# Decay attention with a soft mixture of experts on one core: score tiles of 64x128, row-group sums in 128x32 tiles, C's transposes as filler

## Chip, cores and metric

One core of one Trainium2 chip. The metric is device time in microseconds (us) of one execution; of several executions the median is given.

## What is computed

Four batches, 8 heads of 64 columns, 768 positions, all in f32. For each head and each block of positions the reference computes

    intra = (q k^T * Dmask) v          Dmask[i, j] = lam^(i-j) for i >= j
    inter = (q * lam^(pos+1)) kv_state
    out   = intra + inter
    kv_state = lam^block * kv_state + (k * lam^(block-1-pos))^T v

and then, with x the attention output as 3072 rows of 512 columns, a soft mixture of 8 experts with 4 slots each:

    logits = x phi                                   (3072 x 32)
    d = softmax of logits over the rows, slot_input = d^T x   (32 x 512)
    slot_out[e] = relu(slot_input[e] w1[e]) w2[e]    (w1: 512 x 1024, w2: 1024 x 512 per expert)
    c = softmax of logits over the slots, result = c slot_out

## The kernel before

The host only lays the inputs out. The kernel works with blocks of 128 positions: 24 tiles t (6 per batch), taken as 12 pairs u = (a, b) by the loop at L482. Every engine runs its instructions in the order in which the code is written (`InOrder`), and nearly all of them carry the line of that helper, L48; so the profile is read by the names of tiles.

One pair, on TensorE (PE), in this order: `scores(a)` (q k^T of 8 heads: 16 matmuls into banks sc0 and sc1), `recall(a)` (the state's part: 8 matmuls into xa and xb, from `qs` and `st`), `scores(b)` (banks tr and dp), `recall(b)`, `natural` of the two tiles before (8 transposes), `turn_k` (up to 8 transposes of k), in every second pair `weights` (2 transposes), `attend` (masked scores times v: 8 matmuls into xa, then 8 into xb), `gathered` (k^T v for the state: up to 16 matmuls into bank kv), and then `logits` (odd pairs, 16 matmuls) or `slots` (even pairs, 4). VectorE (DVE) masks the scores (`at`) and carries the state (`st`); GpSimd (POOL) makes `qs`, the decayed state `dec` and `vd`; ScalarE (ACT) copies results out of PSUM. A matmul of f32 is run as two passes: two matmul records and two weight loads in the trace; a transpose is one of each.

Tiles of the array: a matmul with 64 rows of contraction and 64 output columns uses a quarter of the array, and four such run beside each other; the scores and the recall are both of this form (64*64 in the trace). `natural` and `turn_k` are 128*128, `attend` and `gathered` 128*64, `logits`, `slots` and both expert layers 128*32 (four expert groups beside each other), the last products with C 32*128 (four row groups).

Loads are issued by SyncE (SP) alone: the q, k, v tiles of pair u+2 during pair u (14 buffers `ld`), and between them 3.4 tiles of w1 per pair (512 KB each, 32 buffers `slab`); w2 follows as buffers come free.

After the last pair comes a chain (L570 to L767) with filler transposes `busy(n)`, which do no work and stand where PE would wait: the maximum over the four row groups of 32 partitions (`cm`, a matmul with `blk`, a 128x128 tile made of four copies of `sel`), the slot weights `selw`, the slot inputs `si` (8 matmuls into one bank, then three transposes by DVE into `e`), `first(Q)` for the two halves of the experts (32 matmuls each, kc by kc; `between` is called after the second of four kc), the softmax denominators `den`, the last group of C (`lp`, `slot_softmax`, then six transposes `turn_C` inside `first(1)`), and the second layer: `second(0)` and `second(1)` with 16 calls of `quad` each (4 matmuls). Into `second(1)` are put `spread(0)` (the slot outputs of the first 256 columns, summed over row groups with `blk`) before quad `AT_SPREAD`, and three `put` (8 matmuls with C for 1024 rows each, copied out by ACT and DVE and stored) before the quads `AT_PUTS`. Then `spread(1)` and three `put` of the second half end the kernel. `put` takes its four banks from a list of seven in turn.

    AT_SPREAD = 2
    AT_PUTS = (5, 9, 13)

Of the kernel before, what the change touches and what calls it, by code (L numbers as in the profile page):

```python
# [8 lines left out]
F32 = mybir.dt.float32  # L9
# [19 lines left out]
HD = D // 2  # L29
NU = T // 2  # L30

AT_SPREAD = 2
AT_PUTS = (5, 9, 13)
AHEAD = 20
PACE = 34

# [17 lines left out]
def decay_attn_soft_moe(  # L54
# [153 lines left out]
    def scores(t, tags):  # L208
        q_, k_ = IN[t, 0], IN[t, 1]
        SC[t] = [bank(tag) for tag in tags]  # L210
        for hp in range(HP):
            for j in range(2):
                for hh in range(2):
                    r = slice(64 * hh, 64 * hh + 64)
                    pe.matmul(
                        out=SC[t][hh][64 * j:64 * j + 64, hp * P:(hp + 1) * P],
                        lhsT=k_[r, hp * P + 64 * j:hp * P + 64 * j + 64],
                        rhs=q_[r, hp * P:(hp + 1) * P],
                        start=True,
                        stop=True,  # L220
                    )
        AT[t] = []

    def masked(t, hh):
# [63 lines left out]
                    skip_group_check=True,  # L288
                )

    def attend(ts, xt):
        for hh in range(2):
            for t in ts:
                v_ = IN[t, 2].rearrange("p (h c) -> p h c", h=H)
                for hp in range(HP):
                    pe.matmul(
                        out=place(t, hh, hp),
                        lhsT=v_[:, HP * hh + hp, :],
                        rhs=AT[t][hh][:, hp, :],
                        start=False,  # L300
                        stop=True,
                        skip_group_check=True,
                    )
            banks, at = XB[ts[0]]
            n = 2 * P * len(ts)
            act.copy(
                out=xt[:, ts[0] % 2:ts[-1] % 2 + 1, 2 * hh:2 * hh + 2],
                in_=banks[hh][:, at:at + n].rearrange("p (t a b) -> p t a b", t=len(ts), a=2),
            )
        for t in ts:  # L310
            XT[t] = xt[:, t % 2]
# [20 lines left out]
    def carry(t, kv):  # L332

        if not has_state(t):
            return
        n = t % NB
        st = work.tile([P, HP, DH], F32, tag="st", name="st", bufs=2)
        if n == 0:
            dve.tensor_copy(out=st, in_=kv)
        else:  # L340
            dve.tensor_tensor(out=st, in0=DEC[t - 1], in1=kv, op=ALU.add)
        ST[t] = st
# [135 lines left out]
        dve.tensor_reduce(out=gsel, in_=ident.rearrange("p (g s) -> p g s", g=4), axis=AX.X, op=ALU.add)  # L478

    ask = sm = late_sums = iter(())  # L480
    kv = None
    for u in range(NU):  # L482
        a, b, c = 2 * u, 2 * u + 1, 2 * u + 2
        opens, last = a % NB == 0, u == NU - 1
        feed(u)
        if u == NU - 2:
            for _ in range(NLOAD - 6):
                load_one(*ld1)
        if last:
            for tag, n in (("kn", 2), ("vd", 1)):  # L490
                for _ in range(n):
                    load_one(work, tag, n)

        scores(a, ("sc0", "sc1"))
        if u > 0:
            carry(a, kv[:, 1])
            decay_state(a)
        masked(a, 0)
        masked(a, 1)
        xb = [bank("xa"), bank("xb")]  # L500
        XB[a], XB[b] = (xb, 0), (xb, 2 * P)
        if u == 0:
            decay_v(0)
            decay_q(1)
            turn_k(0, "gl", True)
            scores(b, ("tr", "dp"))
            kv = gathered((0,))
            carry(0, kv[:, 0])
            decay_state(0)
            masked(b, 0)  # L510
            masked(b, 1)
            turn_k(b, "sc0", True)
            turn_k(c, "sc1", False)
            decay_v(b)
            decay_q(c)
            recall(b, True)
        else:
            if not opens:
                recall(a, True)
            scores(b, ("tr", "dp"))  # L520
            masked(b, 0)
            masked(b, 1)
            recall(b, opens)
            next(ask, None)
            next(ask, None)
            next(late_sums, None)
            decay_v(b)
            if u == 1:
                place_phi()
            decay_q(c)  # L530
            natural(a - 2, "sc0")
            natural(a - 1, "sc1")
            if not last:
                turn_k(b, "tr", True)
                turn_k(c, "dp", False)
            if u % 2 == 0:
                sm = slot_softmax(u // 2 - 1, weights("gl"))
                next(sm)
            decay_q(c + 1)
        xt = keep.tile([P, 2, HP, P], F32, tag="xt", name="xt", bufs=2)  # L540
        attend((a, b), xt)
        next(sm, None)
        if u == 0:
            constants()
        if not last:
            kv = gathered((b, c))
            carry(b, kv[:, 0])
            decay_state(b)
            if u == 0:
                decay_q(c + 1)  # L550
        next(sm, None)
        if u % 2 == 1:
            ask = logits(u // 2)
            next(ask)
            if not last:
                next(ask)
        elif u > 0:
            late_sums = slots(u // 2 - 1)
            next(late_sums)
# [7 lines left out]
    for _ in range(2):  # L567
        load_two(keep, "xt", 2)

    def busy(n):  # L570

        idle = bank("tr")
        for _ in range(n):
            pe.transpose(idle[:, 0:P], ident, ident)

    negm = run["m"]
    blk = work.tile([P, 4, SL], F32, tag="st", name="blk", bufs=2)
    blk_ = blk.rearrange("p g s -> p (g s)")
    pool.tensor_copy(out=blk, in_=sel.rearrange("p (o s) -> p o s", o=1).broadcast_to([P, 4, SL]))
    dve.tensor_scalar(out=gm, in0=gsel, scalar1=negm, scalar2=None, op0=ALU.mult)  # L580
    natural(T - 2, "tr")
    next(ask)
    natural(T - 1, "dp", dve.tensor_copy)
    cm = bank("kv")
    pe.matmul(out=cm[:, 0:4], lhsT=blk_, rhs=gm, start=True, stop=True)
    weights("xb", raw=False, copy=dve.tensor_copy)
    busy(6)
    dve.tensor_reduce(out=own, in_=cm[:, 0:4], axis=AX.X, op=ALU.min)
    wgt = small.tile([P, 1], F32, tag="mx", name="wgt")
    act.activation(out=wgt, in_=negm, func=AF.Exp, bias=own, scale=-1.0)  # L590
# [2 lines left out]
    pool.tensor_scalar(out=selw, in0=sel, scalar1=wgt, scalar2=None, op0=ALU.mult)  # L593
    late_sums = slots(G - 1, ("sc0", "sc1"))
    next(late_sums)
    busy(2)
    next(late_sums)
    for _ in range(4):
        load_one(keep, "x", 4)

    si = bank("xa")
    for half in range(2):
        for kc in range(4):
            pe.matmul(
                out=si[SL * kc:SL * kc + SL, half * DH:(half + 1) * DH],
                lhsT=selw,
                rhs=acc[:, half * HD + kc * DH:half * HD + (kc + 1) * DH],
                start=True,
                stop=True,
            )  # L610

    busy(4)
    sT = e.rearrange("p (a b) -> p a b", a=4)
    for cols in (slice(0, SL), slice(SL, DH), slice(DH, P)):
        dve.transpose(out=e[:, cols], in_=si[:, cols])
    next(ask)
    wl = small.tile([P, 1], F32, tag="rs", name="wl")
    dve.tensor_tensor(out=wl, in0=wgt, in1=lsum, op=ALU.mult)
# [1 line left out]
    rown = small.tile([P, 2], F32, tag="rown", name="rown", bufs=1)  # L620

    def denominators():
        den = bank("kv")
        pe.matmul(out=den[:, 0:1], lhsT=blk_, rhs=wl, start=True, stop=True)
        dve.tensor_scalar(out=rden, in0=den[:, 0:1], scalar1=1e-9, scalar2=None, op0=ALU.add)
        dve.reciprocal(out=rden, in_=rden)

        dve.tensor_tensor(out=rown, in0=own2, in1=rden.broadcast_to([P, 2]), op=ALU.mult)
# [59 lines left out]
            quad(d_, Q, f, w, n == 0, n == len(todo) - 1)  # L688

    first(0, denominators)  # L690
    lp = bank("dp")[:, 0:P]
    pe.transpose(lp, L, ident)
    while late:
        load_two()
    for x in slot_softmax(G - 1, lp):
        pass
    CT = slabs.tile([P, G, P], F32, tag="slab", name="CT")

    def turn_C():

        tops = [bank("sc0"), bank("sc1")]
        for g in range(G):
            pe.transpose(
                tops[g // 3][:, (g % 3) * P:(g % 3 + 1) * P],
                CN[:, 4 * g:4 * g + 4, :].rearrange("p g s -> p (g s)"),
                ident,
            )
        for i, copy in enumerate((act.copy, dve.tensor_copy)):
            copy(out=CT[:, 3 * i:3 * i + 3, :], in_=tops[i][:, 0:3 * P].rearrange("p (a b) -> p a b", a=3))

    first(1, turn_C)

    so = work.tile([P, D], F32, tag="at", name="so", bufs=4)
    po1 = bank("xa")
# [10 lines left out]
    def spread(half):  # L725

        rep = bank(("gl", "xb")[half])
        pe.matmul(out=rep[:, 0:HD], lhsT=blk_, rhs=so[:, half * HD:(half + 1) * HD], start=True, stop=True)
        x = slabs.tile([P, HD], F32, tag="slab", name="s4")
        split(x, rep)  # L730
        s4.append(x)
# [25 lines left out]

    second(0, po, {})
    split(so[:, 0:HD], po)
    fill = {AT_SPREAD: lambda: spread(0)}  # L760
    for i, n in enumerate(AT_PUTS):
        fill[n] = lambda i=i: put(i, 0)
    second(1, po1, fill)
    split(so[:, HD:D], po1)
    spread(1)
# [59 lines left out]
```

## Time and profile before

| | |
|---|---|
| median of 3 runs | 164.79 us (164.21 to 165.23) |
| the profiled execution, its own time | 164.39 us |
| its span, first to last instruction | 162.6 us |
| mean granted TensorE clock, share of full | 0.987 |
| PE busy | 146.9 us (90%) |
| HBM read, written | 52.50 MB, 6.29 MB |

The span leaves 1.8 us of the profiled execution outside. PE is PE's matmuls, PEld its weight loads. A matmul record lasts longer than the distance to the next one, since they are pipelined; what the stream costs is read from the starts. "issue" names time in which an engine waited for nothing that the profile shows.

### The profile page before, as it was taken

The numbers are of one execution on the slowest core, as the hardware profiler recorded it, in microseconds if no ns is written. First come the engines' busy times: TensorE is split into PE (matmuls) and PEld (weight loads), VectorE is DVE, ScalarE is ACT, GpSimd is POOL, SyncE is SP. The second block draws the span as 40 slices with busy tenths as digits, with TensorE's granted clock in tenths as the row PEclk, the third lists the DMA queues.
The fourth block names the chain that finished last, engine by engine and source line by source line (L and its number), as shares of the span: only waits on it lengthen the run. The fifth ranks groups of instructions, "written<-read, shape, count | busy, mean of one in ns | idle before, by whom it ended". The sixth has DMA issues, their size and how long they took to land.

```text
span 162.6 us, 6432 instructions
## 1 busy us (share of the span) xinstructions
PE 146.9 (90%) x2768; PEld 111.6 (69%) x2768; DVE 81.3 (50%) x184; ACT 49.2 (30%) x112; POOL 48.7 (30%) x64
## 2 busy tenths in 40 slices
PE   7899996999699999999799999999999999996900
PEld 7688995799597888689779998885333365552600
DVE  1994544573835747573657385735117140334620
ACT  3122431433151335233252436053010200323520
POOL 1286942281733237471329182300000000000000
PEclk9999999999999999999999999999999999999995
DMA  5999999999999799999999995999999999699597
GB/s 179 315 395 406 410 413 404 411 410 404 406 392 360 254 384 401 408 414 404 370 363 397 409 393 176 317 374 403 374 406 408 403 406 403 243 341 364 206 383 258
DMA packets 30748, 59.21 MB, mean 364 GB/s; under 512 B 2944, under 2 KB 9216, under 8 KB 30720
## 3 DMA queue, kind: packets, MB, share of 16 engines
q1 hardware_dynamic: 30576, 58.80, 95.8%
q8 instruction: 22, 0.36, 0.8%
q14 instruction: 6, 0.05, 0.1%
q10 hardware_dynamic: 144, 0.01, 0.1%
HBM read 52.50 MB, written 6.29 MB: 362 GB/s over the span
## 4 chain that ended last, share of the span: by engine, by line
PE 81%; issue 4%; POOL 4%; DVE 3%; DMA 2%; ACT 1%; DVEq 1%; POOLq 0%; ACTq 0%
PE xa L48 19%; PE sc L48 16%; PE gl L48 12%; PE tr L48 11%; PE kv L48 10%; PE xb L48 9%; PE dp L48 4%; POOL qs L48 2%; DMA lam_sb<-lam_x 2%; DVE mask L48 2%; DVE qpow L48 1%; POOL dec L48 1%; POOL vd L48 1%; DVEq L821 1%; ACT o L48 0%
## 5 line engine op out<-in xcount | busy, mean ns | idle before, releaser
L48 POOL TENSOR_TENSOR qs<-ld,qpow 128x512 f32<-128x512 f32 x20 | 25.4, 1278 | 5.8 <-issue 2.4
L48 ACT COPY x<-sc 128x512 f32<-128x512 f32 x22 | 11.8, 589 | 41.1 <-PE sc L48 41.1
L48 POOL TENSOR_TENSOR dec<-st,qpow 128x256 f32<-128x256 f32 x16 | 10.0, 622 | 33.0 <-DVE st L48 33.0
L48 DVE TENSOR_TENSOR at<-sc,mask 128x512 f32<-128x512 f32 x24 | 15.4, 683 | 5.4 <-PE sc L48 5.4
L48 PE MATMUL tr<-ld 64*64 64x128 f32 x192 | 13.2, 270 | 2.4 <-issue 1.6
L48 DVE TENSOR_TENSOR st<-dec,kv 128x256 f32<-128x256 f32 x16 | 6.7, 419 | 15.7 <-PE kv L48 12.8
L48 PE MATMUL xa<-qs,st 64*64 64x128 f32 x160 | 12.8, 271 | 1.6 <-issue 1.4
L48 PEld LDWEIGHTS sc<-ld 64*64 64x64 f32 x384 | 10.3, 132 | 5.4 <-issue 4.3
L48 PE MATMUL sc<-ld 64*64 64x128 f32 x384 | 13.2, 275 | 0.0
L48 PE MATMUL dp<-ld 64*64 64x128 f32 x192 | 13.2, 271 | 0.0
L48 PE MATMUL xa<-at,ld 128*64 128x128 f32 x192 | 13.2, 279 | 0.0
L48 PEld LDWEIGHTS tr<-ld 64*64 64x64 f32 x192 | 11.1, 133 | 3.0 <-issue 3.0
L48 PE MATMUL sc<-ident,xt 128*128 128x128 f32 x88 | 12.2, 280 | 0.9 <-issue 0.9
L48 PE MATMUL xb<-qs,st 64*64 64x128 f32 x160 | 12.9, 271 | 0.0
L48 PE MATMUL xb<-at,ld 128*64 128x128 f32 x192 | 12.6, 273 | 0.0
L48 PEld LDWEIGHTS xa<-at,ld 128*64 128x64 f32 x192 | 10.3, 136 | 2.0 <-issue 1.7
L48 PEld LDWEIGHTS sc<-ident,xt 128*128 128x128 f32 x88 | 9.5, 141 | 2.9 <-issue 2.7
L48 PEld LDWEIGHTS xa<-qs,st 64*64 64x64 f32 x160 | 9.7, 133 | 2.2 <-issue 1.8
L48 POOL TENSOR_TENSOR vd<-ld,mask 128x512 f32<-128x512 f32 x9 | 9.6, 1062 | 5.1 <-DVE mask L48 5.1
L48 PEld LDWEIGHTS dp<-ld 64*64 64x64 f32 x192 | 11.0, 133 | 0.0
L48 DVE TENSOR_TENSOR kn<-dp,mask 128x512 f32<-128x512 f32 x10 | 6.9, 691 | 8.1 <-PE dp L48 7.1
L48 PEld LDWEIGHTS xb<-at,ld 128*64 128x64 f32 x192 | 10.9, 137 | 0.0
(159 smaller groups left out, 285.0 us busy)
## 6 DMA issues: line engine op xcount, KB each, us to landing
slab<-w_x SPq DMA_DIRECT2D x32, 512.0 KB, 6.9
w2p<-w_x SPq DMA_DIRECT2D x18, 512.0 KB, 10.0
w2t<-w_x SPq DMA_DIRECT2D x28, 256.0 KB, 5.3
ld<-kT SPq DMA_DIRECT2D x24, 256.0 KB, 5.8
ld<-qT SPq DMA_DIRECT2D x24, 256.0 KB, 5.7
ld<-vN SPq DMA_DIRECT2D x24, 256.0 KB, 6.2
y<-o SPq DMA_DIRECT2D x24, 256.0 KB, 2.6
L<-phi_x SPq DMA_DIRECT2D x1, 64.0 KB, 4.6
```

The lines of the kernel that those rows point to most:

```text
L48: return self._tc.keep_in_program_order(f(*args, **kwargs))
L821: with tile.TileContext(nc) as tc:
```

## The change

Scores: one matmul of 64x128 for every head in place of two of 64x64, and `recall(a)` moves behind `scores(b)`.

```diff
         for hp in range(HP):
-            for j in range(2):
-                for hh in range(2):
-                    r = slice(64 * hh, 64 * hh + 64)
-                    pe.matmul(out=SC[t][hh][64 * j:64 * j + 64, hp * P:(hp + 1) * P],
-                        lhsT=k_[r, hp * P + 64 * j:hp * P + 64 * j + 64], rhs=q_[r, hp * P:(hp + 1) * P], ...)
+            for hh in range(2):
+                r = slice(64 * hh, 64 * hh + 64)
+                pe.matmul(out=SC[t][hh][:, hp * P:(hp + 1) * P],
+                    lhsT=k_[r, hp * P:(hp + 1) * P], rhs=q_[r, hp * P:(hp + 1) * P], ...)
...
-            if not opens:
-                recall(a, True)
             scores(b, ("tr", "dp"))
             masked(b, 0)
             masked(b, 1)
+            if not opens:
+                recall(a, True)
```

State: in even pairs `gathered`, `carry` and `decay_state` run between the two halves of `attend`; in odd pairs behind it, as before.

```diff
+        def states():
+            kvs[0] = gathered((b, c))
+            carry(b, kvs[0][:, 0])
+            decay_state(b)
+        attend((a, b), xt, states if u % 2 == 0 else None)
...
+        if u % 2 == 1 and not last:
+            states()
```

The end chain: row-group sums as four 128x32 matmuls with `sel` (`blk` goes); `idle` in place of `busy`, in fewer transposes; four of C's six transposes (written back over `CN`) ahead of `cm`; `lp` moves ahead of the first layer, from bank dp to bank tr; the slot inputs of the second half, their DVE transposes and `den` inside `first(0)`; `turn_C` goes from `first(1)`.

```diff
+    def summed(dst, src):
+        for r in range(4):
+            pe.matmul(out=dst[SL * r:SL * r + SL], lhsT=sel, rhs=src, start=True, stop=True)
...
+    idle(2)
+    for g in range(4):
+        turn_C(top[:, g * P:(g + 1) * P], g)
     cm = bank("kv")
-    pe.matmul(out=cm[:, 0:4], lhsT=blk_, rhs=gm, start=True, stop=True)
-    busy(6)
+    summed(cm[:, 0:4], gm)
...
+    lp = bank("tr")[:, 0:P]
+    pe.transpose(lp, L, ident)
+    idle(2)
...
+    inputs_of(0, "dp")
+    idle(3)
...
     def denominators():
+        inputs_of(1, "dp")
+        den = bank("sc0")
+        summed(den[:, 0:1], wl)
...
     first(0, denominators)
-    lp = bank("dp")[:, 0:P]
-    pe.transpose(lp, L, ident)
...
-    first(1, turn_C)
+    first(1)
```

The last layer: `AT_SPREAD = 1`, `AT_PUTS = (3, 3, 10)`; before quad 3 now stand `last_C` (C's last two transposes into bank xb, and their copy), `put(0)` and `put(1)`.

How the order moves, at three places. First PE in the second pair; sc_325, sc_326 and tr, dp are the score banks of a and b, xa and xb those of the recall. Before:

```order
L48 MATMUL sc_325<-ld 64x128 [waits DMAHW1_49,PE_49]
L48 MATMUL sc_326<-ld 64x128 [waits PE_49]
...
L48 MATMUL xa<-qs,st 64x128 [waits DVE_49,Activation_49,Pool_49]
L48 MATMUL xb<-qs,st 64x128 [waits Activation_49]
...
L48 MATMUL tr<-ld 64x128 [waits DMAHW3_49,DMAHW2_49]
L48 MATMUL dp<-ld 64x128
...
L48 MATMUL xa<-qs,st 64x128 [waits DVE_49,Pool_49]
```

And now, the same banks under the names sc_309 and sc_310 (each name stands for all its matmuls of the step here):

```order
L48 MATMUL sc_309<-ld 128x128 [waits DMAHW1_49,PE_49]
L48 MATMUL sc_310<-ld 128x128 [waits PE_49]
...
L48 MATMUL tr<-ld 128x128 [waits DMAHW3_49,DMAHW2_49]
L48 MATMUL dp<-ld 128x128
...
L48 MATMUL xa<-qs,st 64x128 [waits DVE_49,Activation_49,Pool_49]
L48 MATMUL xb<-qs,st 64x128 [waits Activation_49]
...
L48 MATMUL xa<-qs,st 64x128 [waits DVE_49,Pool_49]
```

Both score steps stand together, of 8 matmuls each and not 16, and both recalls behind them. Second PE where `first(1)` begins (banks xa and tr), before:

```order
L48 MATMUL dp<-ident,L 128x128
L48 MATMUL xa<-slab,e 32x512 [waits PE_49]
L48 MATMUL xa<-slab,e 32x512 x3
L48 MATMUL tr<-slab,e 32x512 [waits PE_49]
L48 MATMUL tr<-slab,e 32x512 x3
```

and now:

```order
L48 MATMUL xa<-slab,e 32x512 [waits Activation_49]
L48 MATMUL xa<-slab,e 32x512 x3
L48 MATMUL tr<-slab,e 32x512 [waits DVE_49]
L48 MATMUL tr<-slab,e 32x512 x3
L48 MATMUL xa<-slab,e 32x512 x3
```

On DVE at that place, now (h and hz are the hidden layer of `first(0)`, cmx and ce the softmax of C's last group):

```order
L48 TENSOR_SCALAR h<-xb,rown 128x512 [waits DMAHW1_49,DVE_49,PE_49]
L48 STREAM_TRANSPOSE hz<-h 128x512 [waits Activation_49]
L48 STREAM_TRANSPOSE hz<-h 128x512 [waits DVE_49]
L48 TENSOR_REDUCE cmx<-tr 128x4
L48 TENSOR_TENSOR ce<-tr,cmx 128x128 [waits DVE_49,Pool_49]
L48 TENSOR_REDUCE cs<-ce 128x4 [waits Activation_49]
```

The order on DVE is as before, but cmx and ce read bank tr where they read dp, and PE's first matmul into tr waits for DVE where it waited for PE itself. Third PE in `second(1)` from quad 3, now (s is the spread first half, CN holds C):

```order
L48 MATMUL xb<-ident,CN 128x128
L48 MATMUL xb<-ident,CN 128x128 [waits Pool_49]
L48 MATMUL tr<-s_2285,CN 128x256 [waits DVE_49]
L48 MATMUL sc_2301<-s_2285,CN 128x256
L48 MATMUL sc_2302<-s_2285,CN 128x256
L48 MATMUL dp<-s_2285,CN 128x256
...
L48 MATMUL kv<-s_2285,CN 128x256 [waits PE_49]
L48 MATMUL gl<-s_2285,CN 128x256 [waits PE_49]
L48 MATMUL xb<-s_2285,CN 128x256 [waits Activation_49]
L48 MATMUL tr<-s_2285,CN 128x256 [waits Activation_49]
```

Two `put` stand back to back, and the second one's last bank is the first one's first, tr, which ACT must have copied out; before, four quads stood between two `put`.

## Rows read from the trace of the kernel before

**Rows 1.** The page, busy time, share and instruction count of PE and its weight loads.

```profile
PE 146.9 (90%) x2768; PEld 111.6 (69%) x2768; DVE 81.3 (50%) x184; ACT 49.2 (30%) x112; POOL 48.7 (30%) x64
```

**Rows 2.** The page, chain that ended last, by engine.

```profile
PE 81%; issue 4%; POOL 4%; DVE 3%; DMA 2%; ACT 1%; DVEq 1%; POOLq 0%; ACTq 0%
```

**Rows 3.** Timeline of PE: start, length, instruction, and idle time before it.

```profile
26.17 0.27 PE L48 MATMUL tr<-ld 64*64 64x128 f32 x1 [1.42 <-issue]
...
44.54 0.32 PE L48 MATMUL xa<-qs,st 64*64 64x128 f32 x1 [1.42 <-issue]
...
80.39 0.71 PE L48 MATMUL sc<-ident,xt 128*128 128x128 f32 x5 [0.88 <-issue]
```

**Rows 4.** The page, a DMA queue: kind, packets, MB, share of 16 engines.

```profile
q8 instruction: 22, 0.36, 0.8%
```

**Rows 5.** Windows: stretch, us, busy (count) by engine, PEclk, DMA share, GB/s.

```profile
26.10:44.40 18.30, 16.95 (x379) 14.64 (x378) 11.23 (x24) 6.24 (x15) 8.04 (x9) 1.00 1.04 408
44.40:63.10 18.70, 18.53 (x378) 16.04 (x378) 10.30 (x23) 7.24 (x18) 6.92 (x8) 1.00 0.94 354
63.10:80.30 17.20, 16.13 (x378) 13.96 (x379) 10.47 (x23) 5.65 (x14) 7.71 (x9) 1.00 1.03 403
...
39.20:43.00 3.80, 3.80 (x131) 3.41 (x126) 2.74 (x7) 0.80 (x4) 2.31 (x4) 1.00 1.04 412
57.70:63.00 5.30, 5.30 (x129) 4.70 (x129) 3.63 (x9) 1.92 (x8) 3.29 (x4) 1.00 1.03 397
```

**Rows 6.** Timeline of PE in pairs 7 and 8, changes of tile form.

```profile
70.46 0.27 PE L48 MATMUL xb<-qs,st 64*64 64x128 f32 x1
70.66 1.09 PE L48 MATMUL sc<-ident,xt 128*128 128x128 f32 x8
...
75.38 1.08 PE L48 MATMUL gl<-xt,phi_sb 128*32 128x128 f32 x32
76.39 1.10 PE L48 MATMUL sc<-ld 64*64 64x128 f32 x32
```

**Rows 7.** Groups by line: weight loads; busy us, mean ns of one.

```profile
L48 PEld LDWEIGHTS sc<-ld 64*64 64x64 f32 x384 | 10.3, 132 | 5.4 <-issue 4.3 <-DMA ld<-vN 0.8
...
L48 PEld LDWEIGHTS sc<-s,CT 32*128 32x128 f32 x32 | 3.7, 184 | 0.8 <-DVE o L48 0.4 <-ACT o L48 0.3
```

**Rows 8.** Timeline of PE, recall of the second pair.

```profile
16.22 0.32 PE L48 MATMUL xa<-qs,st 64*64 64x128 f32 x1 [0.18 <-POOL qs L48]
```

**Rows 9.** Timeline, 113 to 118.2 us: into the first layer, and the denominators.

```profile
114.27 1.06 PE L48 MATMUL gl<-slab,e 128*32 128x512 f32 x8
...
117.84 0.38 PE L48 MATMUL kv<-wl,blk 128*128 128x1 f32 x2
...
118.15 1.06 PE L48 MATMUL gl<-slab,e 128*32 128x512 f32 x8
```

**Rows 10.** Timeline, 121.7 to 126.5 us: from first(0) into first(1).

```profile
121.72 0.33 PE L48 MATMUL dp<-ident,L 128*128 128x128 f32 x1
121.94 0.75 DVE L48 TENSOR_SCALAR h<-xb,rown 128x512 f32<-128x512 f32 x1 [3.13 <-PE xb L48]
...
124.18 0.29 DVE L48 TENSOR_TENSOR ce<-dp,cmx 128x128 f32<-128x128 f32 x1
...
125.55 0.93 PE L48 MATMUL sc<-ident,CN 128*128 128x128 f32 x6
...
126.41 1.06 PE L48 MATMUL xa<-slab,e 128*32 128x512 f32 x8
```

**Rows 11.** Timeline of PE in the second layer and behind it.

```profile
137.75 0.70 PE L48 MATMUL gl<-so,blk 128*128 128x256 f32 x2
138.38 1.50 PE L48 MATMUL xa<-w2p,hz 128*32 128x256 f32 x24
...
150.36 0.48 PE L48 MATMUL gl<-s,CT 32*128 32x256 f32 x1 [0.68 <-DVE s L48]
...
152.16 0.48 PE L48 MATMUL gl<-s,CT 32*128 32x256 f32 x1 [0.23 <-ACT o L48]
```

More of the change, by code (lines that the diff above doesn't have):

```diff
@@ L30 @@
 NU = T // 2
-AT_SPREAD = 2
-AT_PUTS = (5, 9, 13)
+AT_SPREAD = 1
+AT_PUTS = (3, 3, 10)
 AHEAD = 20
@@ L211, in scores @@
         for hp in range(HP):
-            for j in range(2):
-                for hh in range(2):
-                    r = slice(64 * hh, 64 * hh + 64)
[L215 to L221, printed above, removed]
+            for hh in range(2):
+                r = slice(64 * hh, 64 * hh + 64)
+                pe.matmul(
+                    out=SC[t][hh][:, hp * P:(hp + 1) * P],
+                    lhsT=k_[r, hp * P:(hp + 1) * P],
+                    rhs=q_[r, hp * P:(hp + 1) * P],
+                    start=True,
+                    stop=True,
+                )
         AT[t] = []
@@ L289, in recall, with attend @@
                 )
-    def attend(ts, xt):
+    def attend(ts, xt, between=None):
         for hh in range(2):
+            if hh and between is not None:
+                between()
             for t in ts:
@@ L480, in decay_attn_soft_moe @@
     ask = sm = late_sums = iter(())
-    kv = None
+    kvs = [None]
     for u in range(NU):
@@ L495, in decay_attn_soft_moe @@
         if u > 0:
-            carry(a, kv[:, 1])
+            carry(a, kvs[0][:, 1])
             decay_state(a)
@@ L540, in decay_attn_soft_moe @@
         xt = keep.tile([P, 2, HP, P], F32, tag="xt", name="xt", bufs=2)
-        attend((a, b), xt)
+        def states():
[3 more added lines that the diff above has]
+        attend((a, b), xt, states if u % 2 == 0 else None)
         next(sm, None)
@@ L544, in decay_attn_soft_moe @@
             constants()
[L545 to L550, printed above, removed]
+        if u % 2 == 1 and not last:
+            states()
+        if u == 0:
+            decay_q(c + 1)
         next(sm, None)
@@ L568, in decay_attn_soft_moe, with idle, turn_C @@
         load_two(keep, "xt", 2)
-    def busy(n):
-        idle = bank("tr")
+    CT = CN.rearrange("p (g c) s -> p g (c s)", g=G)
+    top = bank("xa")
+    def idle(n):
         for _ in range(n):
-            pe.transpose(idle[:, 0:P], ident, ident)
+            pe.transpose(top[:, 0:P], ident, ident)
+    def turn_C(dst, g):
+        pe.transpose(dst, CN[:, 4 * g:4 * g + 4, :].rearrange("p g s -> p (g s)"), ident)
     negm = run["m"]
-    blk = work.tile([P, 4, SL], F32, tag="st", name="blk", bufs=2)
-    blk_ = blk.rearrange("p g s -> p (g s)")
-    pool.tensor_copy(out=blk, in_=sel.rearrange("p (o s) -> p o s", o=1).broadcast_to([P, 4, SL]))
+    def summed(dst, src):
+        for r in range(4):
+            pe.matmul(out=dst[SL * r:SL * r + SL], lhsT=sel, rhs=src, start=True, stop=True)
     dve.tensor_scalar(out=gm, in0=gsel, scalar1=negm, scalar2=None, op0=ALU.mult)
@@ L583, in decay_attn_soft_moe @@
     natural(T - 1, "dp", dve.tensor_copy)
+    weights("xb", raw=False, copy=dve.tensor_copy)
+    idle(2)
+    for g in range(4):
+        turn_C(top[:, g * P:(g + 1) * P], g)
     cm = bank("kv")
-    pe.matmul(out=cm[:, 0:4], lhsT=blk_, rhs=gm, start=True, stop=True)
-    weights("xb", raw=False, copy=dve.tensor_copy)
-    busy(6)
+    summed(cm[:, 0:4], gm)
     dve.tensor_reduce(out=own, in_=cm[:, 0:4], axis=AX.X, op=ALU.min)
@@ L595, in decay_attn_soft_moe, with inputs_of @@
     next(late_sums)
-    busy(2)
+    act.copy(out=CT[:, 0:4, :], in_=top.rearrange("p (a b) -> p a b", a=4))
     next(late_sums)
+    top = bank("kv")
+    lp = bank("tr")[:, 0:P]
+    pe.transpose(lp, L, ident)
+    idle(2)
     for _ in range(4):
         load_one(keep, "x", 4)
-    si = bank("xa")
-    for half in range(2):
+    def inputs_of(half, tag):
+        si = bank(tag)[:, 0:DH]
         for kc in range(4):
             pe.matmul(
-                out=si[SL * kc:SL * kc + SL, half * DH:(half + 1) * DH],
+                out=si[SL * kc:SL * kc + SL],
                 lhsT=selw,
@@ L610, in decay_attn_soft_moe @@
             )
-    busy(4)
+        for x in range(2):
+            at = slice(SL * x, SL * x + SL)
+            dve.transpose(out=e[:, half * DH + SL * x:half * DH + SL * x + SL], in_=si[:, at])
+    inputs_of(0, "dp")
+    idle(3)
     sT = e.rearrange("p (a b) -> p a b", a=4)
-    for cols in (slice(0, SL), slice(SL, DH), slice(DH, P)):
-        dve.transpose(out=e[:, cols], in_=si[:, cols])
     next(ask)
@@ L622, in denominators @@
     def denominators():
-        den = bank("kv")
-        pe.matmul(out=den[:, 0:1], lhsT=blk_, rhs=wl, start=True, stop=True)
+        inputs_of(1, "dp")
+        den = bank("sc0")
+        summed(den[:, 0:1], wl)
         dve.tensor_scalar(out=rden, in0=den[:, 0:1], scalar1=1e-9, scalar2=None, op0=ALU.add)
@@ L696, in decay_attn_soft_moe @@
         pass
[L697 to L709, printed above, removed]
-    first(1, turn_C)
+    first(1)
     so = work.tile([P, D], F32, tag="at", name="so", bufs=4)
@@ L727, in spread @@
         rep = bank(("gl", "xb")[half])
-        pe.matmul(out=rep[:, 0:HD], lhsT=blk_, rhs=so[:, half * HD:(half + 1) * HD], start=True, stop=True)
+        summed(rep[:, 0:HD], so[:, half * HD:(half + 1) * HD])
         x = slabs.tile([P, HD], F32, tag="slab", name="s4")
@@ L759, in decay_attn_soft_moe, with last_C @@
     split(so[:, 0:HD], po)
+    def last_C():
+        top = bank("xb")
+        for g in (4, 5):
+            turn_C(top[:, (g - 4) * P:(g - 3) * P], g)
+        act.copy(out=CT[:, 4:6, :], in_=top[:, 0:2 * P].rearrange("p (a b) -> p a b", a=2))
     fill = {AT_SPREAD: lambda: spread(0)}
-    for i, n in enumerate(AT_PUTS):
-        fill[n] = lambda i=i: put(i, 0)
+    for n in set(AT_PUTS):
+        fill[n] = lambda n=n: [put(i, 0) for i in range(3) if AT_PUTS[i] == n]
+    fill[AT_PUTS[0]] = lambda f=fill[AT_PUTS[0]]: [last_C(), f()]
     second(1, po1, fill)
```

## The prediction

> **What bounds the kernel now.** I read the page first, then the chain, PE's own waits, and then windows and timelines of the stretches that the change touches. PE is busy for 90% of the span with 2768 matmul records and as many weight loads [rows 1], and the chain that ended last runs through PE for 81%, with "issue" (waits for nothing that the profile shows) next at 4% [rows 2]. So the kernel costs what PE's stream costs, plus the places where PE is held.
>
> Up to 105 us, where the pairs end, three holds stand out, and no semaphore explains them: they fall in the middle of a row of like matmuls, with 1.42, 1.42 and 0.88 us of idle time [rows 3]. A record lasts 0.27 us while the next one starts 0.11 us later (five in 0.71 us), so a hold is 0.16 us longer in the stream than the idle time says: 1.58, 1.58, 1.04 us. A fourth, small one ends the second stretch of rows 5 (18.53 of 18.70 us busy, so 0.17, or 0.3 in the stream). Together 4.5 us.
>
> What they are: one queue moved 22 packets of instructions, 0.36 MB [rows 4], and 5536 instructions of PE over 22 packets make 252, or 126 matmul records with their loads. Between the ends of the holds lie 379, 378 and 378 matmuls [rows 5], each time three packets. And the last packet before a hold was used up fast: 39.2 to 43.0 us, 131 matmuls and 126 loads, in 3.8 us with a hold of 1.6, and 57.7 to 63.0 us, 129 and 129, in 5.3 us with a hold of 0.3 [rows 5]. My reading: a packet is fetched when the one before it is begun and takes 5.2 to 5.6 us to come, through DMA engines that are full (408 GB/s [rows 5]); PE is held where it uses 126 matmuls up in less. The densest places are the pairs' recalls and 64x64 scores, four matmuls per 0.11 us.
>
> **The change, part by part.** The sum is made against the profiled execution (164.39 us, 0.40 under the median of the runs).
>
> *Scores.* Each tile's scores go from 16 matmuls (32 records) to 8 (16 records). 32 records of 64x64 run four beside each other, 16 of 64x128 two: in both cases eight rounds of 0.107 us, so the array gains nothing. What goes is instructions: by the printed order, the matmul records of a pair fall from 182 to 150 on average. The densest 126 in a row are then 32 of `gathered` (0.92 us), 32 of `logits` (0.86), 32 of scores (2 x 0.86), 30 of recall (0.8), and four changes of tile form (0.4): 4.7 us against 3.8 now. Counting packets through the new order, one packet of the eleven ends there (in pair 10); the others have over 6.2 us. One hold of 0.5 us in place of 4.5: -4.0 us. Bounds: -4.5, and +0.5 if the fetch does not go by density (rival B).
>
> *A change of tile form more per pair.* Scores and recall were both 64*64; now 64*128 goes to 64*64. Where the form changes, the stream shows a gap: recall's last start at 70.46 us, the transposes at 70.66 instead of 70.57; 32 logits records from 75.38 end at 76.24, scores start at 76.39 [rows 6]: 0.09 and 0.15 us. No row shows this very change; below it is nothing, above 0.15. I take 0.1, the nearest row, in eleven pairs: +1.1 us (0 to 1.6). `recall(a)` was moved so that it is one change and not three.
> The Trainium skill says that changing the tiling mode, and not just the tile, drains the engine (TensorEngine Tiling (Array Packing), Key Properties). By that the new change of form must cost like the others; without it, the 1.1 us would fall away.
>
> *Weight loads.* A load of 64 columns takes 132 ns, one of 128 columns 184 ns [rows 7], so 128 columns take about 104 ns of loading against a round of 107: just hidden. Up to 0.05 us a tile if it isn't quite: +0.2 us (0 to 1.2).
>
> *State between the halves of `attend`.* In the first pair this brings `st` 0.9 us forward, and POOL's chain behind it, for which recall waited at 16.22 us [rows 8]. PE's own work then reaches that recall at 15.9: -0.3 us (0 to -0.5). In later pairs nothing waited for the state; nothing gained. The copy of the second half comes 0.9 us later and is needed three steps later: hidden.
>
> *Into the first layer.* It starts at 114.27 us [rows 9], behind eight slot-input matmuls, their transposes and fillers. `cm` stands behind seven transposes now, so `selw` comes 0.5 us later, still ahead of the sums that are late. `first(0)` needs half the inputs, and starts at 113.6: -0.65. The other half stands in `first(0)` with its DVE transposes directly ahead of the matmuls that read them: matmul to transpose to matmul takes 0.7 us, against 0.42 for `den` now (0.31 from its start to the next matmul [rows 9], and a gap ahead): +0.3.
>
> *`lp` and `turn_C`.* The `lp` transpose and its changes of form cost 0.37 us of PE, C's six transposes 125.44 to 126.41, 0.97 us [rows 10]. Both go from here: -1.3 us. The four C transposes in front take the place of fillers, so they cost nothing.
>
> *What is late next.* `lp` now lies in bank tr, and `first(1)` writes its second 16 records into tr. Its readers, cmx and ce, stand on DVE behind h and two transposes of `first(0)`. PE ends `first(0)` at 121.6 by these rows; DVE starts h at 121.94 and ends ce at 124.47 [rows 10], and PE has it some 0.15 us later: 3.0 us after the end of `first(0)`, of which 16 records into xa fill 0.86. PE stands for 2.15 us: +2.15 (1.8 to 2.5). Queued behind it is all the rest of PE's work.
>
> *Second layer.* `spread(0)` one quad (0.43 us) earlier waits for `so`, and saves its changes of form: now 137.64 to 138.38, quads 0 and 1 done [rows 11]; then 138.15 with one done: +0.2. `last_C`: two transposes and a change of form, +0.3. Two `put` back to back: the tail shows them now. The first starts at 150.36 us; the second's last bank is the first's first, and waits for its copy until 152.16 [rows 11], where 151.24 would be its turn: 0.9 lost, less 0.35 for two changes of form saved: +0.5. Together +1.0 us (0.5 to 1.5).
>
> *Tail.* `spread(1)` without the 128*128 load: -0.1.
>
> Sum: -4.0 + 1.1 + 0.2 - 0.3 - 0.65 + 0.3 - 1.3 + 2.15 + 1.0 - 0.1 = -1.6 us. In the pairs -3.0, behind them +1.4. Against the median: 164.79 - 1.6 = 163.2 us.
>
> **Rivals.**
> B, *every third packet holds PE, dense or not* (slower). The distances of 378 matmuls are exactly three packets, and a packet trio may be fetched only when PE has nearly run out. If it is asked for 64 instructions before the end and takes 2.5 us, the four holds fit as well (0.9 us of work left and 1.6 held; 2.4 and 0.3). The new order puts such ends behind sparse work once and behind recall, `logits` and recall in the other cases: 0.3 + 1.5 + 1.4 + 1.3 = 4.5 us, nothing gained: -1.6 + 4.0 = +2.4, 167.2 us. It decides wherever holds come 378 matmuls apart again. Against it: three packets are two pairs now, so like places come round by themselves.
> The Trainium skill gives TensorE a queue 64 deep (TensorE: Matmul & The Clock Gate, Architectural detail), which would fit a fetch that starts 64 instructions early; no row shows the queue.
> C, *the loads give the gain back*. A pair loads six tiles of 256 KB and 3.4 of 512 KB, 3.36 MB, 8.2 us at 408 GB/s, and PE needs 8.7 us a pair now (378 matmuls in 18.07, 182 a pair), 8.4 then. At 390 GB/s it is 8.6, and of 3.0 us some 1.8 are lost: 165.0 us. For it: full DMA. Against: 354 GB/s in the second stretch [rows 5], so there is room, and PE waits for no load after the start.
> D, *the new score tiles run slower*: loads not quite hidden (1.2 in place of 0.2) and changes of form at 0.15 (1.6 in place of 1.1): +1.5 us, 164.7. For it: a load of 104 ns in a round of 107 has no room. Against: loads and matmuls run beside each other in every step now.
> That the 2.15 us are not there is hardly possible: DVE's order and the bank are printed.
>
> **How the numbers follow.** The reading above 0.56, B 0.17, C 0.15, D 0.12. The first one's own range is 161.6 to 164.6; C and D lie within 1%, B above. 1% (1.65 us) is about what a measurement of this kernel can tell from no change. The first case's sum lies just on that edge (163.15), and what is least sure in it, the wait at tr (taken near its upper bound) and the changes of form, would rather move it down: three quarters of it, 0.42, below the edge, the rest within 1%; of C and D 0.03 below it. Of B 0.16 is above the other edge (166.4), 0.01 within. So faster 0.45, same 0.39, slower 0.16. The range leaves out the upper half of B and the tail below: 161.2 to 166.8 us.
>
> **What would show it.** Right: PE's "issue" idle of 1 us and more gone up to 103 us; `first(1)` with a PE wait of some 2 us on DVE ce; the gap between scores and recall near 0.1 us; `put` 1 waiting for ACT. Wrong: holds of over 1 us again 378 matmuls apart (B); PE waiting for ld (C); score rows more than 0.95 us apart (D); or no wait at tr.

## The result, and the profile after

The changed kernel takes 162.24 us (median of 4 runs, 162.07 to 162.42), 0.985 of the time before (interval 0.981 to 0.989). The profiled execution took 162.07 us with a span of 160.3: 2.3 us less than the one before. The kernel before varies more from execution to execution (162.94 to 169.21 us in 14 runs beside the experiments) than the changed one (0.35 us in these four), so the ratio compares the faster executions of both, and no trace shows what makes the others slower.

The page of the changed kernel (PE and its loads, the chain, the instruction queue; compare [rows 1, 2, 4]):

```profile
PE 145.9 (91%) x2403; PEld 111.3 (69%) x2403; DVE 81.3 (51%) x184; ACT 49.4 (31%) x113; POOL 48.4 (30%) x63
...
q8 instruction: 19, 0.31, 0.8%
...
PE 85%; DVE 5%; DMA 2%; ACT 1%; issue 1%; DVEq 1%
```

The chain's "issue" fell from 4% to 1%, and DVE rose. Windows place this, first of the kernel before, then of the changed one: pairs 2 to 10 (counted from 0), and, after the change alone, from the last pair to the first layer, `first(0)`, `first(1)` and the second half of the second layer (columns as in [rows 5]):

```profile
22.56:102.16 79.60, 75.57 (x1659) 65.43 (x1655) 46.32 (x103) 29.10 (x71) 33.85 (x38) 1.00 0.98 378
```

```profile
22.41:98.22 75.81, 75.81 (x1371) 65.56 (x1367) 47.04 (x104) 28.98 (x71) 34.36 (x39) 1.00 1.01 394
98.22:109.89 11.67, 11.53 (x194) 9.12 (x190) 6.12 (x16) 4.30 (x11) 0.58 (x2) 1.00 0.99 347
109.89:117.50 7.61, 7.25 (x82) 2.38 (x85) 0.91 (x7) 0.61 (x1) 0.00 (x0) 1.00 1.05 400
117.50:126.44 8.94, 7.06 (x68) 1.98 (x64) 3.06 (x8) 0.91 (x3) 0.40 (x1) 1.00 1.05 405
...
133.35:146.65 13.30, 12.08 (x191) 6.71 (x183) 4.74 (x9) 4.39 (x10) 0.00 (x0) 1.00 0.92 333
```

In these nine pairs PE stood for 4.03 us before and for nothing now: not one hold is left in them, with 288 records fewer. `first(1)` holds 1.88 us of standing, and the second layer's half 1.22. PE's waits after the change (us in total, times, longest) name them:

```profile
PE tr L48 <- DVE ce L48: 1.9, 1, 1.9
...
PE xb L48 <- DVE so L48: 0.7, 1, 0.7
...
PE gl L48 <- DVE e L48: 0.4, 1, 0.4
PE gl L48 <- DVE so L48: 0.3, 1, 0.3
...
PE tr L48 <- ACT o L48: 0.2, 1, 0.2
```

The largest is the one forecast at tr. In the timeline eight records into xa start, then PE waits behind DVE's row, h, hz, cmx, ce:

```profile
117.50 1.04 PE L48 MATMUL xa<-slab,e 128*32 128x512 f32 x8
120.41 1.06 PE L48 MATMUL tr<-slab,e 128*32 128x512 f32 x8 [1.88 <-DVE ce L48]
```

```profile
117.83 0.75 DVE L48 TENSOR_SCALAR h<-xb,rown 128x512 f32<-128x512 f32 x1 [3.31 <-PE xb L48]
118.49 1.29 DVE L48 STREAM_TRANSPOSE hz<-h 128x512 f32<-128x512 f32 x2
119.71 0.25 DVE L48 TENSOR_REDUCE cmx<-tr 128x4 f32<-128x128 f32 x1
120.07 0.29 DVE L48 TENSOR_TENSOR ce<-tr,cmx 128x128 f32<-128x128 f32 x1
```

### The profile page after: what moved, and what is told of

Read it like the earlier page. It is cut to its first block, busy times and chain, and to the rows that moved or that the text cites. A ratio compares the mean times of both kernels' runs of the same rounds, so it can differ in the third digit from the quotient of the medians.

```text
span 160.3 us, 5707 instructions
## 1 busy us (share of the span) xinstructions
PE 145.9 (91%) x2403; PEld 111.3 (69%) x2403; DVE 81.3 (51%) x184; ACT 49.4 (31%) x113; POOL 48.4 (30%) x63
## 4 chain that ended last, share of the span: by engine, by line
PE 85%; DVE 5%; DMA 2%; ACT 1%; issue 1%; DVEq 1%
PE xa L48 20%; PE sc L48 17%; PE tr L48 12%; PE gl L48 12%; PE kv L48 10%; PE xb L48 10%; PE dp L48 3%; DMA lam_sb<-lam_x 2%; DVE mask L48 2%; DVE qpow L48 1%; DVE hz L48 1%; ACT o L48 1%; DVEq L836 1%; DVE h L48 0%; DVE so L48 0%
## 5 line engine op out<-in xcount | busy, mean ns | idle before, releaser
L48 PEld LDWEIGHTS sc<-ld 64*128 64x128 f32 x192 | 11.6, 187 | 5.5 <-issue 5.4
L48 PE MATMUL sc<-ld 64*128 64x128 f32 x192 | 13.9, 285 | 0.0
L48 PE MATMUL tr<-ld 64*128 64x128 f32 x96 | 12.7, 273 | 0.7 <-DMA ld<-kT 0.7
L48 PE MATMUL dp<-ld 64*128 64x128 f32 x96 | 12.7, 273 | 0.0
L48 PEld LDWEIGHTS tr<-ld 64*128 64x128 f32 x96 | 11.6, 188 | 0.9 <-DMA ld<-qT 0.9
L48 PEld LDWEIGHTS dp<-ld 64*128 64x128 f32 x96 | 11.6, 188 | 0.0
L48 PE MATMUL xa<-qs,st 64*64 64x128 f32 x160 | 11.4, 277 | 0.0
L48 PE MATMUL xb<-qs,st 64*64 64x128 f32 x160 | 11.4, 277 | 0.0
L48 PEld LDWEIGHTS xa<-qs,st 64*64 64x64 f32 x160 | 8.5, 132 | 1.5 <-issue 0.2
```

The costliest lines, as they stand in the source:

```text
L48: return self._tc.keep_in_program_order(f(*args, **kwargs))
```

## The experiments

Each ratio is to the kernel before, run beside the experiment on the same chip. The changed kernel was not run there again, so what is said against it rests above all on the lengths of stages in the two profiles.

**scores_only.** Is the gain the scores' alone? The kernel before, with `scores` as in the change, and:

```diff
-            if not opens:
-                recall(a, True)
             scores(b, ("tr", "dp"))
...
+            if not opens:
+                recall(a, True)
             recall(b, opens)
```

> The kernel before with nothing but the scores in 64x128 tiles and recall(a) behind them. My reading: all of the gain lies in the pairs, and the rest of the change costs 1.4 us. So the last pair's scores start at about 98.4 us (102.16 before), no idle time is put down to issue in the pairs, the part behind the pairs is as long as before, and the profiled time is 160.6 to 160.9, below that of the full change (162.07). Rival, that the gain in the pairs also needs the state between the halves of attend: pairs 1 us or more longer than that. Rival B of the prediction: holds of over 1 us every 378 matmul records, 164 us or more.

161.03 us median, ratio 0.979 (0.976 to 0.982); profiled span 159.2. Pairs 2 to 10:

```profile
22.71:98.55 75.84, 75.84 (x1371) 66.10 (x1367) 46.47 (x103) 28.88 (x71) 33.90 (x38) 1.00 1.02 394
```

As long as in the full change, with no standing. From the last pair's first score to the end it takes 60.7 us, the kernel before 60.4 and the full change 62.1. This one edit beats the full change by 1.2 us (medians): all that it gains lies in the pairs, and the rest of the change costs. Its second pair takes 9.19 us (8.75 in the full change); of these 0.4 us some 0.1 are a wait for POOL's `qs`, and the rest lies where a packet ends.

**lp_bank.** Is the wait at tr the bank's doing? The changed kernel, and:

```diff
-    lp = bank("tr")[:, 0:P]
-    pe.transpose(lp, L, ident)
     idle(2)
...
     inputs_of(0, "dp")
-    idle(3)
+    lp = bank("sc1")[:, 0:P]
+    pe.transpose(lp, L, ident)
+    idle(2)
```

> The changed kernel with the lp transpose in bank sc1 and not in tr, behind the first slot inputs, in place of one filler. My reading: first(1) waits for DVE's ce only because tr holds lp. PE's wait at tr (2.03 us in the stream) goes, first(1) takes 6.9 us and not 8.94, and the profiled time falls from 162.1 to about 160.1. Rival: something else of the second layer is then late (hz, or the weights of the second layer still on their way), a new wait of 1 us or more stands at the head of second(0) or between its quads, and under 1 us is gained.

160.21 us (160.1 expected), ratio 0.973 (0.971 to 0.976). The records into tr now start 0.86 us behind those into xa:

```profile
117.91 1.04 PE L48 MATMUL xa<-slab,e 128*32 128x512 f32 x8
118.77 1.04 PE L48 MATMUL tr<-slab,e 128*32 128x512 f32 x8
...
123.92 1.04 PE L48 MATMUL tr<-slab,e 128*32 128x512 f32 x8
124.77 0.60 PE L48 MATMUL kv<-w2t,hz 128*32 128x256 f32 x6
```

`first(1)` takes 6.86 us in place of 8.94, and no new wait stands in the second layer. The rival falls.

**less_load.** What makes a packet late? The kernel before, and:

```diff
-        want = min(NSLAB, (AHEAD + u * PACE) // 10)
+        want = min(NSLAB, 8 * max(0, u - 7))
```

> The kernel before, with the loads of the first layer's weights all put off to the last four pairs: up to the eighth pair only the inputs are loaded, some 190 GB/s and not 400. Later parts become slow and are not looked at. My reading, a packet comes late because it passes through full DMA engines: the holds of 26.2 and 44.5 us (1.6 and 1.8 us) and the small ones up to 70 us shrink to under 0.5 us each or go. Rival: a packet takes its 5.2 to 5.6 us whatever the DMA engines do (or every third packet holds PE): both holds stand as they were, within 0.3 us.

Pairs 2, 4 and 7 in windows, of the kernel before and then of this one:

```profile
22.56:32.17 9.61, 8.19 (x171) 6.63 (x167) 5.58 (x14) 3.33 (x9) 2.28 (x4) 1.00 1.04 408
40.28:50.84 10.56, 9.14 (x190) 7.65 (x186) 5.75 (x15) 3.91 (x11) 4.74 (x6) 1.00 1.01 393
67.28:76.39 9.11, 8.94 (x212) 8.09 (x208) 4.76 (x8) 2.73 (x5) 5.10 (x7) 1.00 1.04 408
```

```profile
22.61:30.59 7.98, 7.98 (x171) 6.56 (x167) 5.59 (x14) 3.32 (x9) 2.29 (x4) 1.00 0.58 190
38.71:47.91 9.20, 9.14 (x191) 7.65 (x187) 5.76 (x15) 3.91 (x11) 4.71 (x6) 1.00 0.58 189
64.00:72.52 8.52, 8.52 (x213) 7.92 (x209) 4.76 (x8) 2.73 (x5) 5.11 (x7) 1.00 0.69 191
```

The same records at half the DMA rate: 1.6, 1.4 and 0.6 us less. Of the hold at pair 4's recall 0.48 us is left (recall takes 1.03 us, 0.55 where nothing holds it), the other two are gone. By these windows pair 7 had a hold of 0.6 us that the prediction did not list. (This kernel's one run took 184.13 us.) Later in the same run the put-off loads come, and with them a hold in pair 9, where the kernel before had none: its window, and PE's row.

```profile
80.56:90.09 9.53, 8.62 (x197) 7.65 (x193) 4.25 (x7) 2.73 (x5) 4.46 (x5) 1.00 1.03 409
```

```profile
89.67 0.49 PE L48 MATMUL gl<-xt,phi_sb 128*32 128x128 f32 x9 [0.91 <-issue]
```

The trace also has the packets themselves, in DMA queue q8, 16 KB each. The one whose absence held PE until 26.17 us before was moved from 23.92 to 24.88 us, beginning 3.1 us after the first record of the packet ahead of it; here the same packet's transfer begins at 21.01 us, 0.1 us after that record. The queue from 23.9 to 24.9 us before, and from 20.9 to 21.9 us here:

```profile
q8 instruction: 1, 0.02, 6.0%
```

```profile
q8 instruction: 1, 0.02, 8.0%
```

Over pairs 2 to 10 of the kernel before, a transfer begins 1.2 to 3.8 us after the first record of the packet ahead (2.9 on average) and takes 0.9 us; here, up to pair 7, it begins 0.0 to 1.7 us after it (0.65) and takes 0.9 to 2.0 us. The holds end 1.3 to 1.5 us after a transfer's end, in both. So full DMA engines are what delays a packet, and the delay lies ahead of its transfer.

**shifted.** Do holds follow the program or the packets? The kernel before, and:

```diff
-NWARM = 9
+NWARM = 6
...
         pe.matmul(out=wps[:, 0:P], lhsT=warm[:, 0:P], rhs=warm[:, 0:P], start=True, stop=True)
+    for i in range(43):
+        r = SL * (i % 4)
+        pe.matmul(out=wps[r:r + SL, 0:1], lhsT=warm[:, 0:SL], rhs=warm[:, 0:1], start=True, stop=True)
```

> The kernel before, its program unchanged but for the warming up: three 128-column matmuls fewer, 43 tiny ones more (160 instructions of PE more in front), so that every instruction packet ends 80 matmul records earlier in the program. My reading, holds where 126 records are used up in less than some 5.2 us: the holds of 26.2, 44.5 and 80.4 us go; what is left are smaller ones where a packet now ends (about 0.2 to 0.7 us each at scores of the sixth pair, 0.0 to 0.5 at the transposes of the ninth, 0.5 to 1.0 at recall of the eleventh, counted from one), 1.0 to 2.5 us together and not 5.4; profiled time 161.5 to 163. Rival B, every third packet holds PE: holds of 1 to 1.6 us 378 records apart as before, 4 to 5 us together, 164 us or more.

Ratio 0.997 (0.987 to 1.006); the profiled execution took 164.51 us. The three old holds are gone, and new ones stand in the fourth, eighth and eleventh pair (3, 7 and 10 from 0); 0.4 us more are lost in the sixth:

```profile
35.42 0.44 PE L48 MATMUL sc<-ident,xt 128*128 128x128 f32 x2 [0.62 <-DVE at L48]
...
70.75 0.49 PE L48 MATMUL sc<-ident,xt 128*128 128x128 f32 x3 [0.82 <-DVE at L48]
...
94.49 0.27 PE L48 MATMUL xb<-qs,st 64*64 64x128 f32 x1 [1.10 <-issue]
```

(The first two are put down to DVE's `at`, which had ended 0.6 and 1.8 us earlier: the held instruction carries a wait, so the profile names that. The place called the ninth pair in the expectation is this eighth one, miscounted.) So holds stand where packets end: each of these ends 1.2 to 1.5 us after the transfer of a packet. But the one in the fourth pair was not expected, and pairs 2 to 10 take 78.14 us, 3.9 above the 74.2 that they take without holds, not 1.0 to 2.5, and the time is rival B's. The four held records stand 378, 378 and 504 records apart, so their spacing alone does not decide against B; the transfers in less_load do, which begin within 1.7 us of the first record of the packet ahead and not near its end. A packet's time to come is not 5.2 to 5.6 us each time: from the first record of the packet ahead to the held one it is 5.0 to 6.0 us for the eight clearest holds of the two traces. What sets that spread was not tried.

**recall_back.** What does a change of tile form cost? The changed kernel, and:

```diff
+            if not opens:
+                recall(a, True)
             scores(b, ("tr", "dp"))
...
-            if not opens:
-                recall(a, True)
             recall(b, opens)
```

> The changed kernel with recall(a) back between the two score tiles of a pair, which in eight pairs makes two changes of tile form more, 16 in all. My reading after the result: scores and recall take 3.02 us a pair in place of 2.79, of which 0.15 is the change of form (a gap of 0.09 and a slow start of 0.06) and 0.08 the pace of the 64x128 tiles. So each of these pairs takes 0.3 us longer and the kernel 2.4 us: profiled time 164.5. By the 0.1 us of the prediction: 1.6 us, 163.7. Rival, that the change of form costs nothing and all of the 0.23 us is the tiles' pace: no difference, 162.1.

165.11 us (ten runs, 164.93 to 165.41), ratio 1.002 (0.999 to 1.005). Timeline of PE, pair 7: recall to scores and on:

```profile
67.18 0.27 PE L48 MATMUL xb<-qs,st 64*64 64x128 f32 x1
67.38 0.37 PE L48 MATMUL tr<-ld 64*128 64x128 f32 x1
67.39 0.37 PE L48 MATMUL dp<-ld 64*128 64x128 f32 x1
67.60 0.27 PE L48 MATMUL tr<-ld 64*128 64x128 f32 x1
```

A change shows twice: 0.20 us to the next start where 0.11 is the pace, and again 0.22 us from the first to the second. Scores and recall of a pair take 3.38 us (1.09 + 0.60 + 1.09 + 0.60), and 3.02 in the changed kernel: 0.18 us a change, above both figures of the expectation. Holds don't come back in pairs 2 to 10: the score tiles alone remove them.

**puts_apart.** The changed kernel with the second layer's table as before:

```diff
-AT_SPREAD = 1
-AT_PUTS = (3, 3, 10)
+AT_SPREAD = 2
+AT_PUTS = (5, 9, 13)
```

> The changed kernel with the second layer's table as it was (spread before the third quad, puts before quads 5, 9 and 13, counted from 0). My reading: the second half of the second layer takes 12.6 us and not 13.3, PE's waits there for ACT's o (0.23) and DVE's so (0.28) go, and the profiled time is 161.4. Rival, the output's transfers set the end: the later last put sends its four stores later, the tail after the last spread grows by as much, and the time stays at 162.1.

161.16 us, ratio 0.978 (0.972 to 0.983). That half of the second layer takes 12.29 us in place of 13.30, from its first row to the last spread:

```profile
133.50 1.05 PE L48 MATMUL xa<-w2p,hz 128*32 128x256 f32 x16
...
145.79 0.64 PE L48 MATMUL xb<-so,sel 128*32 128x256 f32 x8 [0.71 <-DVE so L48]
```

The table cost 1.0 us, and the transfers don't take it back: the tail behind the last spread is 13.6 us as before.

**combined.** The version that these runs point to, lp_bank and:

```diff
-            if between is not None and kc == 1:
+            if between is not None and kc == 0:
...
-AT_PUTS = (3, 3, 10)
+AT_PUTS = (4, 8, 12)
...
-    fill = {AT_SPREAD: lambda: spread(0)}
+    fill = {AT_SPREAD: lambda: [last_C(), spread(0)]}
...
-    fill[AT_PUTS[0]] = lambda f=fill[AT_PUTS[0]]: [last_C(), f()]
```

> The changed kernel with lp in sc1 (as in lp_bank), the second slot inputs one step of the first layer earlier (so that their DVE transposes lie beside its second step), C's last two transposes ahead of the first spread, where PE waits, and the puts before quads 4, 8 and 12. My reading, term by term: -2.0 (wait for ce), -0.3 (wait for e), -0.4 (C's transposes), -0.5 (put waiting for put): 158.9 us. Rival, the loads of the second layer's weights or the output's transfers are late by then: a wait for w2t or w2p of 0.5 us or more, or a tail longer than 13.6 us after the last spread, and 159.5 to 160.2.

159.18 us (158.81 to 160.00), ratio 0.966 (0.959 to 0.973), the fastest of all, and between the 158.9 expected and the rival's 159.5; no wait for w2t or w2p shows, the tail is 13.75 us. `first(0)` takes 7.07 us (7.61), `first(1)` 6.86 (8.94), the half of the second layer 12.38 (13.30). The profiled execution, the slowest of the four, waited longer for its first loads (0.7 us in the changed kernel):

```profile
PE tr L48 <- DMA ld<-kT: 1.6, 1, 1.6
```

Its second pair takes 9.17 us (8.75): there recall is held for 0.4 us, 1.3 us after a packet's transfer ended. So the new tiles do not exclude a hold everywhere.

## Why the prediction was right or wrong

The time was 162.2 where 163.2 stood, inside the likeliest case's own range, and the ratio's interval (up to 0.989) lies on the faster side of the 1% edge, which had 0.45. Place by place, from like starts in the two timelines of PE. The last pair's first scores, its transposes behind recall and the last transposes, before:

```profile
102.16 1.10 PE L48 MATMUL sc<-ld 64*64 64x128 f32 x32
104.94 1.09 PE L48 MATMUL sc<-ident,xt 128*128 128x128 f32 x8
109.67 0.60 PE L48 MATMUL dp<-ident,xt 128*128 128x128 f32 x4
```

and now, with the start of `first(0)`:

```profile
98.22 1.16 PE L48 MATMUL sc<-ld 64*128 64x128 f32 x16
101.24 1.09 PE L48 MATMUL sc<-ident,xt 128*128 128x128 f32 x8
105.97 0.60 PE L48 MATMUL dp<-ident,xt 128*128 128x128 f32 x4
109.89 1.07 PE L48 MATMUL gl<-slab,e 128*32 128x512 f32 x8
```

- *Pairs*: -3.7 (their last transposes start at 105.97 and not 109.67), forecast -3.0. Three terms were too small, with opposite signs, so that they partly cancel: that the sum came this close is in part luck.
  - *Holds*: -5.4 and not -4.0. They were 5.4 us (the one at 44.5 us took 1.8, pair 7 had 0.6; missed because idle put down to "issue" [rows 3] was read and the lengths of pairs weren't); and the half microsecond forecast to remain did not show: the packet of pair 10 was used up in 5.0 us (4.7 forecast), but its transfer began 1.9 us after the first record of the packet ahead and ended 2.1 us before its turn.
  - *A change of tile form more per pair*: 0.18 us and not 0.1, 2.0 in eleven pairs: only the gap ahead was counted, not the slow start behind. The Trainium skill's rule that changing the tiling mode drains the engine (TensorEngine Tiling (Array Packing), Key Properties) agrees with the trace here, in that each change costs time; what the engine does meanwhile the trace does not show.
  - *Weight loads*: scores and recall of a pair took 2.79 us (2.78 in the rows above) and now take 3.02; less the change, 0.05 a pair, 0.5 in all and not 0.2. That the loads cause it is only argued.
  - *The rest*: some 0.4 us less, which were not forecast, are mostly shorter transposes behind recall (in three pairs 1.03 us where no hold covers it, now 0.93). Rival D was thus right about the tiles (its sign, score rows over 0.95 us apart, is there: 0.99), whose cost the holds more than paid.
- *State between the halves*: the wait for `qs` ahead of the second pair's recall, 0.36 us in the stream before, is gone; forecast -0.3. (With the new tiles alone, in scores_only, some 0.1 of it was left.) That pair is 0.2 us shorter than before (8.75 for 8.93) with the new tiles' 0.23 in it.
- *Into the first layer*: 3.92 us from those transposes to `first(0)`, 4.60 before: -0.68, forecast -0.65. Inside it, slot inputs and `den`: +0.27, forecast +0.3 (the 0.7 us from matmul to transpose to matmul, which stood there without a row, was 0.69: 113.35 to 114.04 us).
- *`lp` and `turn_C`, what is late next*: `first(0)`'s end to `first(1)` -0.37 and C's transposes -0.97, both as forecast; the wait 2.03 us in the stream, forecast 2.15.
- *Second layer*: +1.1, forecast +1.0; of it the table 1.0 by puts_apart. *Tail*: nothing, forecast -0.1.

Behind the pairs that makes +1.4, as forecast. B's period of three packets fell: pairs 2 to 10 have no hold here, nor in five more kernels with these tiles, and the packets are fetched one at a time (less_load). C fell: the pairs move 394 GB/s, and PE waits for no load there. The reading took a packet's time as fixed, 5.2 to 5.6 us; it depends on the DMA engines' load, and at full load it still varied (shifted), so where a hold falls and how long it is was forecast only roughly.

## What to carry to other kernels

Where one engine's stream is dense, count its instructions: a larger tile that does the same work in fewer of them can pay although it runs slower itself (here 0.23 us a pair lost, 5.4 us of holds gone). Price a change of tile form as gap and slow start together. Before a bank is used for a small early result, look up which engine reads it and what stands ahead of that reader: a free choice of bank was worth 2 us here.

## What was not expected of the hardware

A packet of PE's instructions (252 per packet) moved in 0.9 us, but with DMA at about 400 GB/s a held one let PE go on only 5.0 to 6.0 us after the first record of the packet ahead. At 190 GB/s packets used up in 3.7 to 3.8 us led to a hold of 0.5 us once and none the other time.
